# Moving P chunks, a GpSimd copy, two adds and the tail's units in a fused attention and GELU kernel on one core

## Chip, cores and metric

One core of one Trainium2 chip runs the whole kernel. The metric is the device time of an execution in microseconds (us); the kernel before has a median of 205.42 us over three runs. The engines are TensorE (PE, matrix multiply), VectorE (DVE), ScalarE (ACT), GpSimd (POOL) and SyncE (SP, which here only issues DMAs). Each engine works through its own instructions in the order in which the program issues them; semaphores order the engines against each other.

## The reference

Eight batches, eight heads of width 64, 512 tokens `x` and 32 state rows per head. The tokens read from the state and the state reads from the tokens, each through a softmax; the rows of both reads go through a two-layer network with an exact GELU.

```python
scores = x @ state.T / sqrt(D);  a  = softmax(scores);  xread = a  @ state
scores2 = state @ x.T / sqrt(D); a2 = softmax(scores2); sread = a2 @ x
y = concat([xread, sread], axis=2)          # heads side by side: (B*544, 512)
out = gelu(y @ w_in) @ w_out                # w_in 512x2048, w_out 2048x512
```

The inputs and the output (4352 x 512) are float32; matmul operands are cast to bfloat16.

## The kernel before

**The first layer.** `state @ w_in` is computed once for each batch: that is P, 256 rows (head and state row, as two halves `t` of 128) by 2048 columns. `p_mm(b, f)` makes one chunk `f` of 512 columns with eight small matmuls into two PSUM banks (L441); casts move the two halves into `Ps[b]`: `p_copy` puts one on ACT and one on DVE, `p_copy_s` both on ACT, `p_all` splits four chunks between them. The hidden layer of a batch's tokens is then `a @ P`, in 16 units M of 128 hidden columns: `mm1` (two matmuls into a bank `hp`, L506; GELU on ACT, L513, into `gs[b]`). Units 0 to 3 need chunk 0, 4 to 7 chunk 1, 8 to 11 chunk 2, 12 to 15 chunk 3.

**The second layer.** `g @ w_out` is split into 2 x 2 blocks and done with seven products in place of eight, named "1" to "7". Products 5, 6, 7 and 3 need sums of blocks of g, which `g_sum` makes on DVE (L613, tile `gsum`, from the pool `apool` of three buffers); the differences of `w_out` (`w_diff`) are made once. `X(b, name)` does one product: 16 matmuls into a PSUM bank `xp` (L623). `BANK` says which: 1, 6 and 7 accumulate in bank 1, 5 and 3 in bank 2, 2 in bank 0, 4 in bank 3. Since products share a bank, its contents are taken out in between: ACT snapshots (`snap`: c2 after 2, u after 6, s5 after 5, c4 after 4) and DVE adds (`add`, L642), which write the output tile `oh` of the upper or lower half of the tokens. After product 1 the upper half's left columns are done, after 7 both column halves of the lower one, after 3 the upper half's right columns; `x_out` sends them from SP.

**The order.** For batches 2 to 7 a loop of eight slots `p` writes the order out by hand. Each slot does two M units of batch b. Slots 0 to 3 also do products 1, 6, 5 and 7 of batch b-1. Slot 5 does product 3 of b-1, the sread matmuls of batch b (tile `sr`, L877), all four P chunks of batch b+1 (`p_all`) and product 2 of b; slot 7 does product 4 of b. Batch 2's own P is made piecemeal: chunks 0 and 1 ahead of the loop, chunk 2 in slot 0 and chunk 3 in slot 3. Slot 1 holds the scores of batch b+1, slots 2 and 3 the two halves of its softmax division (`norm`, DVE), slot 5 its transpose by DMA (`atr_dma`, SP).

**x.** `load_x` casts and loads x of a batch by a DMA issued from POOL; `hold_for` is a tiny POOL copy that waits for a GELU and so delays what follows it on POOL. From the loaded tile POOL makes two arrangements: `rearr` (L225, for the transposed x, which `xtr_dma` makes from SP) and `rearr_ones` (L235, tile `xo`, the right side of the sread matmuls). There are two `xo` buffers, for even and odd batches, and two buffers `xb`. In batch 2 `rearr_ones(3)` stands in slot 5, `load_x(5)` with its hold in slot 6, `rearr_ones(4)` in slot 7.

**The last batch.** The 256 sread rows of all batches go through both layers together, within slots of batch 7. `read_out_slot` (slots 0 to 4) does their first layer in seven products `SR` for each of two halves `g`, beside the products of batch 6; product SR("7") accumulates in the bank of SR("1") after a DVE add has read it. `R` does their second layer (L847), in slots 5 to 7 and the tail: R's 1, 6 and 7 share one bank, which before is `o1`, the home of `xp`'s bank 1. After the loop the tail does batch 7's products 1, 5 (`L5`), 6, R's 3, then 7 and 3 (`L3`). `l_mm` does 5 and 3 in three pieces in banks 2, 0 and 3, so that the last adds and output pieces can start early.

Of the kernel before, what the change touches and what calls it, by code (L numbers as in the profile page):

```python
# [17 lines left out]
def kernel(  # L18
# [8 lines left out]
    nc = tc.nc  # L27
# [202 lines left out]
    def rearr_ones(b):  # L230
        A = atts[b]
        eng = nc.vector if b < 2 else nc.gpsimd
        src = xbs[b].rearrange("p (t c) (j d) -> p t c j d", t=2, d=D)
        for t in range(2):
            eng.tensor_copy(  # L235
                out=A.xo[:, :, :, 2 + 64 * t:66 + 64 * t].rearrange("p j c d -> p c j d"),
                in_=src[:, t],
            )
# [216 lines left out]
    def pmat(b, f):  # L455
        p_copy(b, f, p_mm(b, f, ftile))
# [124 lines left out]
    xs = {}  # L581
# [53 lines left out]
    def x_out(b, h, ns=slice(None)):  # L635
        rows = out[b * SB:b * SB + S, :].rearrange("(p j) n -> p j n", j=SJ)
        nc.sync.dma_start(out=rows[:, 2 * h:2 * h + 2, ns], in_=xs[b, "o", h][:, :, ns])
# [3 lines left out]
    def add(out, x, y):  # L641
        nc.vector.tensor_tensor(out=out, in0=x, in1=y, op=ALU.add)  # L642
# [5 lines left out]
    def X(b, name):  # L648
        bank = BANK[name]
        first = name in "2154"  # L650
        if first:
            xs[b, bank] = otile([128, 2, NH], "xp", bank)
        ps = xs[b, bank]
        x_mm(ps, x_lhs(b, name), w_rhs(name), first)
        if name == "2":
            if b > 1:
                snap(b, "c2", "c2", ps)
        elif name == "4":
            snap(b, "c4", "c4", ps)
        elif name == "1":  # L660
            for h in range(2):
                xs[b, "o", h] = hpool.tile([128, 2, d_model], FP32, name="oh", tag=f"oh{h}")
            add(xs[b, "o", 0][:, :, left], ps, xs[b, "c2"])
            x_out(b, 0, left)
        elif name == "6":
            snap(b, "u", "u", ps)
        elif name == "5":
            snap(b, "s5", "s5", ps)
        elif name == "7":
            add(xs[b, "o", 1][:, :, right], ps, xs[b, "s5"])  # L670
            add(xs[b, "o", 1][:, :, left], ps, xs[b, "c4"])
            x_out(b, 1)
        elif name == "3":
            add(xs[b, "o", 0][:, :, right], ps, xs[b, "u"])
            x_out(b, 0, right)

    def rows_out(h, js, ns, eng):
        b = B - 1
# [25 lines left out]
    def L5():  # L704
        b = B - 1
        xs[b, "s5"] = c_tile("s5")
        for ps, j, n0, n1 in l_mm("5", True):
            nc.scalar.copy(out=xs[b, "s5"][:, j, n0:n1], in_=ps)

    def L3():  # L710
        b = B - 1
# [121 lines left out]
    def R(name):  # L833
        def c_new(n):
            rs[n] = cpool.tile([128, NH], FP32, name="r_" + n, tag="r_" + n)
            return rs[n]

        bank = BANK[name]
        first = name in "2154"
        if first:  # L840
            home = {"2": 1, "4": 2, "1": 1}
            rs[bank] = otile([128, NH], "rp", home[name]) if name in home else ftile([128, NH], "rp")
        ps = rs[bank]
        lhs = chain(name, r_q, {})[0] if name in "124" else rs["lhs"][name]
        rhs = w_rhs(name)
        for m in range(MH):
            nc.tensor.matmul(  # L847
                ps,
                lhsT=lhs[:, m, :],
                rhs=rhs[:, m, :],  # L850
                start=(first and m == 0),
                stop=(m == MH - 1),
                skip_group_check=True,
            )
        snaps = {"2": "c2", "4": "c4", "6": "u", "5": "s5"}
        if name in snaps:
            nc.scalar.copy(out=c_new(snaps[name]), in_=ps)
        elif name == "1":
            for h in range(2):
                rs["o", h] = opool.tile([128, d_model], FP32, name="osb", tag="osb")  # L860
            add(rs["o", 0][:, left], ps, rs["c2"])
        elif name == "7":
            add(rs["o", 1][:, right], ps, rs["s5"])
            add(rs["o", 1][:, left], ps, rs["c4"])
            r_out(1)
        elif name == "3":
            add(rs["o", 0][:, right], ps, rs["u"])
            r_out(0)
# [49 lines left out]
    def p_copy_s(b, f, ps):  # L918
        for t in range(2):
            nc.scalar.copy(out=Ps[b][:, t, f * 512:(f + 1) * 512], in_=ps[t])  # L920
# [9 lines left out]
    def M(*ms):  # L930
        for m in ms:
            mm1(m // MC, m % MC)
# [5 lines left out]
    def read_out_slot(p):  # L938
        c, b, k = B - 2, B - 1, 16 * (B - 1) + 2 * p
        if p == 0:  # L940
            sr_x("34")
            M(k, k + 1)
            g_sum(c, "56")
            SR("3", 0)
            SR("4", 0)
            X(c, "1")
            sr_x("167")
            SR("5", 0)
            SR("2", 0)
            sr_w("7")  # L950
        if p == 1:
            M(k, k + 1)
            SR_gelu("52", 0)
            X(c, "6")
            SR("1", 0)
            SR("6", 0)
        if p == 2:
            M(k, k + 1)
            SR_gelu("6", 0)
            SR("7", 0)  # L960
            SR_gelu("7", 0)
            g_sum(c, "7")
            X(c, "5")
            SR("3", 1)
            SR("4", 1)
            g_sum(c, "3")
        if p == 3:
            M(k, k + 1)
            SR("5", 1)
            SR("2", 1)  # L970
            SR_gelu("52", 1)
            X(c, "7")
            SR("1", 1)
            SR("6", 1)
        if p == 4:
            M(k, k + 1)
            SR_gelu("6", 1)
            SR("7", 1)
            SR_gelu("7", 1)
            X(c, "3")  # L980
# [146 lines left out]
    for b in range(2, B):  # L1127
        nb = b + 1
        for p in range(8):
            k = 16 * b + 2 * p  # L1130
            if p == 1 and nb < B:
                scores(nb, 0)
                scores(nb, 1)
            if p in (2, 3) and nb < B:
                norm(nb, p - 2)
            if p == 3 and nb + 1 < B:
                xtr_dma(nb + 1)
            if p == 5 and nb < B:
                atr_dma(nb)
            if nb == B and p < 5:  # L1140
                read_out_slot(p)
                if p == 4:
                    r_homes()
                    r_sum("56")
                continue
            M(k, k + 1)
            if b == 2 and p == 0:
                pmat(2, 2)
            if b == 2 and p == 3:
                p_copy_s(2, 3, p_mm(2, 3, ftile))  # L1150
            if b == 2 and p == 1:
                w_diff("7")
            if p < 5 and nb < B:
                if p == 0:
                    g_sum(b - 1, "56")
                if p == 2:
                    g_sum(b - 1, "7")
                if p == 3:
                    g_sum(b - 1, "3")
                if p < 4:  # L1160
                    X(b - 1, "1657"[p])
                if p == 1 and b > 2:
                    sr_w("5216"[b - 3])
            if p == 0 and b + 3 < B:
                hold_for(b, 0)
                load_x(4 if b == 2 else b + 3)
            if p == 6 and b == 2:
                hold_for(b, 12)
                load_x(5)
            if p == 0 and nb + 1 < B:  # L1170
                begin(nb + 1)
                rearr(nb + 1)
            if nb == B:
                if p == 5:
                    R("2")
                    r_sum("73")
                    R("4")
                if p == 6:
                    R("1")
                    X(b, "2")  # L1180
                    R("6")
                    R("5")
                if p == 7:
                    R("7")
                    X(b, "4")
                continue
            if p == 5:
                X(b - 1, "3")
                reads = (b, nb) if nb == B - 1 else (b,)
                p_all(nb, reads)  # L1190
                if b == 2:
                    rearr_ones(3)
                elif nb + 1 < B:
                    rearr_ones(nb + 1)
                X(b, "2")
            if p == 7:
                if b == 2:
                    rearr_ones(4)
                srts(reads)
                X(b, "4")  # L1200
    b = B - 1
    g_sum(b, "56")
    X(b, "1")
    g_sum(b, "73")
    L5()
    X(b, "6")
    R("3")
    X(b, "7")
    L3()


# [28 lines left out]
```

## Time and profile before

| what | value |
| --- | --- |
| time, median of three runs | 205.42 us (205.41 to 206.08) |
| the profiled execution: its time and its span | 205.37 us, 203.6 us |
| granted TensorE clock in it | 0.999 |
| busy share of DVE and ACT | 70%, 70% |
| PE on lines 623 (products) and 506 (M) in the chain that ended last | 38%, 24% |
| last matmul group, L3: start | 197.45 us |
| last output DMA issued | 199.95 us |

The span runs from the first to the last instruction in the profile; the time of the execution is 1.77 us longer. All times in the text are us from the start of the span. A timeline line gives start, duration, engine, line, operation, output<-inputs by their names, shapes and count, and in brackets the idle time of the engine before it with what ended that. Consecutive instructions of one kind are merged, and the ends of matmuls are modelled, so a group can seem to overlap the next one: the distance from start to start says more. A line of waits gives who waited for whom: total us, times, longest. The slices of time list busy time and count of PE, PE's weight loads, DVE, ACT and POOL, then PE's clock, the share of the DMA engines, and GB/s.

### The profile page before, as it was taken

The page shows a single profiled execution, that of the slowest core. Times are in us where ns is not written, and L with a number is a line of the kernel's source. Part 1 is how long each engine was busy: PE and PEld are TensorE (multiplying, and loading weights), DVE is VectorE, ACT ScalarE, POOL GpSimd, SP SyncE. Part 2 cuts the span into 40 slices and gives each one's busy share as a digit, 9 for nine tenths or more (in the row PEclk, how much of TensorE's full clock was granted, in tenths as well). Part 3 has the DMA queues.
Part 4 walks back from the last instruction along what each step waited for, and adds up shares of the span by engine and source line. Part 5 has one row for each costly group of instructions (what it writes and reads, how often), then busy time and mean ns, then how long its engine had stood idle before and what let it go on. Part 6 is the DMA issues. An engine that isn't in the chain of part 4 may idle for free.

```text
span 203.6 us, 4865 instructions
## 1 busy us (share of the span) xinstructions
PE 195.5 (96%) x2035; PEld 133.9 (66%) x2035; DVE 142.7 (70%) x233; ACT 143.3 (70%) x261; POOL 51.5 (25%) x63
## 2 busy tenths in 40 slices
PE   7899999999899999999999999999999999999991
PEld 2434544465667686677777677677766878778991
DVE  2954866788896599856895677567936787860942
ACT  3785677798976889668967796679849488654210
POOL 8963503324266095031504300300000000000000
PEclk9999999999999999999999999999999999999999
DMA  6999999978747979970797033611073010210224
GB/s 197 195 168 203 208 196 202 199 130 152 87 93 159 154 95 152 118 208 1 83 177 209 0 95 65 173 37 53 0 130 82 0 52 3 103 55 0 70 80 163
DMA packets 40166, 23.16 MB, mean 114 GB/s; under 512 B 21840, under 2 KB 38608, under 8 KB 40144
## 3 DMA queue, kind: packets, MB, share of 16 engines
q1 hardware_dynamic: 25472, 14.36, 30.5%
q0 software_dynamic: 13984, 8.10, 29.6%
q10 hardware_dynamic: 688, 0.39, 0.6%
q8 instruction: 16, 0.26, 0.5%
q14 instruction: 6, 0.05, 0.1%
HBM read 17.30 MB, written 8.91 MB: 129 GB/s over the span
## 4 chain that ended last, share of the span: by engine, by line
PE 84%; DVE 4%; DMA 4%; ACT 3%; issue 2%; DVEq 0%; POOL 0%; ACTq 0%; POOLq 0%
PE xp L623 38%; PE hp L506 24%; PE op L548 5%; PE rp L847 3%; PE sp L781 3%; DMA xb<-in_x_dram 3%; DVE oh L642 2%; PE p_ps L441 2%; PE op L532 2%; DMA st_f<-in_state_dram 2%; ACT P L915 1%; PE pt L333 1%; PE sr L877 1%; PE xp L694 1%; PE hp L1022 1%
## 5 line engine op out<-in xcount | busy, mean ns | idle before, releaser
L513 ACT ACTIVATE g<-hp 128x512 bf16<-128x512 f32 x124 | 66.0, 608 | 13.4 <-PE hp L506 13.2
L506 PE MATMUL hp<-AT,P 128*128 128x512 bf16 x248 | 61.2, 379 | 0.0
L623 PEld LDWEIGHTS <-gsum 128*128 128x128 bf16 x416 | 40.4, 98 | 10.3 <-issue 1.2
L623 PE MATMUL xp<-ws,gsum 128*128 128x256 bf16 x320 | 38.2, 273 | 0.9 <-DVE oh L642 0.9
L506 PEld LDWEIGHTS <-P 128*128 128x128 bf16 x248 | 23.4, 98 | 20.9 <-ACT P L452 0.7
L623 PEld LDWEIGHTS <-g 128*128 128x128 bf16 x336 | 32.4, 98 | 6.9 <-issue 1.9
L623 PE MATMUL xp<-w_out_bf,g 128*128 128x256 bf16 x224 | 26.7, 273 | 0.3
L235 POOL COPY xo<-xb 128x1024 bf16<-128x1024 bf16 x12 | 13.6, 1168 | 35.2 <-PE sr L877 35.2
L613 DVE TENSOR_TENSOR gsum<-g 128x2048 bf16<-128x2048 bf16 x14 | 19.0, 1355 | 0.5
L225 POOL COPY x<-xb 128x1024 bf16<-128x1024 bf16 x12 | 14.1, 1211 | 17.3 <-DMA xb<-in_x_dram 17.3
L646 ACT COPY c<-xp 128x512 f32<-128x512 f32 x14 | 8.3, 593 | 9.8 <-PE xp L623 4.5
L623 PE MATMUL xp<-ws,g 128*128 128x256 bf16 x112 | 13.4, 273 | 0.0
L915 ACT CAST P<-p_ps 128x512 bf16<-128x512 f32 x25 | 12.7, 608 | 0.1
L642 DVE TENSOR_TENSOR oh<-xp,u 128x512 f32<-128x512 f32 (+2 forms) x9 | 5.0, 569 | 10.8 <-PE xp L623 10.8
L642 DVE TENSOR_TENSOR oh<-xp,c 128x512 f32<-128x512 f32 x14 | 9.6, 685 | 4.0 <-PE xp L623 4.0
L548 PE MATMUL op<-w_out_bf,g 128*128 128x512 bf16 x48 | 11.8, 380 | 0.0
L623 PE MATMUL xp<-w_out_bf,gsum 128*128 128x256 bf16 x96 | 11.5, 273 | 0.0
L356 DVE TENSOR_TENSOR a<-e,ics 128x512 bf16<-128x512 bf16 x14 | 10.5, 750 | 0.5
L915 DVE CAST P<-p_ps 128x512 bf16<-128x512 f32 x15 | 9.4, 684 | 1.7 <-PE p_ps L441 1.7
L353 DVE TENSOR_REDUCE cs<-e 128x16 f32<-128x512 bf16 x14 | 9.5, 678 | 0.7 <-ACT e L340 0.7
L429 DVE COPY XSR<-srT 128x128 bf16<-128x128 bf16 (+1 forms) x5 | 3.4, 673 | 8.7 <-PE srT L424 8.7
L613 DVE TENSOR_TENSOR gsum<-g,gsum 128x2048 bf16<-128x2048 bf16 x7 | 9.4, 1339 | 0.0
(137 smaller groups left out, 255.4 us busy)
## 6 DMA issues: line engine op xcount, KB each, us to landing
xb<-in_x_dram POOLq DMA_DIRECT2D x7, 512.0 KB, 7.9
out_dram<-oh SPq DMA_DIRECT2D x7, 512.0 KB, 2.8
out_dram<-oh SPq DMA_DIRECT2D x13, 256.0 KB, 2.4
w_in_bf<-in_moe_w_in_dram POOLq DMA_DIRECT2D x6, 256.0 KB, 11.4
out_dram<-osb SPq DMA_DIRECT2D x5, 256.0 KB, 2.9
w_out_bf<-in_moe_w_out_dram POOLq DMA_DIRECT2D x4, 256.0 KB, 8.0
w_out_bf<-in_moe_w_out_dram POOLq DMA_DIRECT2D x2, 512.0 KB, 12.7
x0f<-in_x_dram SPq DMA_DIRECT2D x3, 256.0 KB, 4.0
```

The lines of the kernel that those rows point to most:

```text
L225: nc.gpsimd.tensor_copy(out=A.x4[:, :, :, 64 * t:64 * t + 64].rearrange("p j c d -> p c j d"), in_=src[:, t],)
L235: eng.tensor_copy(out=A.xo[:, :, :, 2 + 64 * t:66 + 64 * t].rearrange("p j c d -> p c j d"), in_=src[:, t],)
L353: nc.vector.reduce_sum(out=cs, in_=e4, axis=AX.X)
L356: nc.vector.tensor_tensor(out=A.a[:, :, hs].rearrange("p g (c n) -> p g c n", n=NS), in0=e4, in1=ics[:, :, :].to_broadcast((128, G, 2, NS) ...
L506: nc.tensor.matmul(hp, lhsT=Ps[b][:, t, m * 128:(m + 1) * 128], rhs=atts[b].AT[:, :, t, :], start=(t == 0), stop=(t == 1),)
L513: nc.scalar.activation(out=gs[b][:, m, :], in_=hp, func=AF.Gelu)
L548: nc.tensor.matmul(ops[b, j], lhsT=gs[b][:, m, j * 128:(j + 1) * 128], rhs=w_out_bf[:, m, :], start=(m == 0), stop=(m == MC - 1),)
L613: nc.vector.tensor_tensor(out=got[name], in0=x, in1=y, op=op)
L623: nc.tensor.matmul(ps[:, j - js[0], :], lhsT=lhs[:, m, 128 * j:128 * j + 128], rhs=rhs[:, m, :], start=(first and j == js[0] and m == 0), ...
L642: nc.vector.tensor_tensor(out=out, in0=x, in1=y, op=ALU.add)
L646: nc.scalar.copy(out=xs[b, name], in_=ps)
L915: copy(out=Ps[b][:, t, f * 512:(f + 1) * 512], in_=ps[t])
```

## The change

- In batch 2's loop, chunk 2 of P leaves slot 0 and chunk 3 leaves slot 3. Slot 2 now does four M units (its own and slot 3's), product 5, the second half of batch 3's `norm` (from slot 3), and then both chunks' matmuls in one run, into the four banks of the pool `f`; ACT casts the first half of each, DVE the second.
- `rearr_ones(4)` goes from slot 7 of batch 2 to slot 5, straight after `rearr_ones(3)`, ahead of `hold_for` and `load_x(5)`.
- Product 7's two adds become `c22` (right columns) and `c21` (left columns). For batches up to 5 they stand where they were. For batch 6, `c21` and the output go behind SR("1") and its add.
- The tail's order becomes 1, R's 7, 6, R's 3, 7, 5, 3. R's 7 comes from slot 7 and R's shared bank moves from `o1` to a bank of `f`. `g_sum` of 7 and 3 are issued apart. The lower half's left columns are added and sent after product 7; its right columns after each half of product 5's pieces, as two DMAs.

```diff
@@ def X
         elif name == "7":
-            add(xs[b, "o", 1][:, :, right], ps, xs[b, "s5"])
-            add(xs[b, "o", 1][:, :, left], ps, xs[b, "c4"])
-            x_out(b, 1)
+            if b < B - 2:
+                c22(b)
+                c21(b)
+                x_out(b, 1)
...
+    def c22(b, js=slice(0, 2)):
+        add(xs[b, "o", 1][:, js, right], xs[b, 1][:, js, :], xs[b, "s5"][:, js, :])
+
+    def c21(b):
+        add(xs[b, "o", 1][:, :, left], xs[b, 1], xs[b, "c4"])
@@ def L5
             nc.scalar.copy(out=xs[b, "s5"][:, j, n0:n1], in_=ps)
+            if n1 == NH:
+                c22(b, slice(j, j + 1))
+                rows_out(1, slice(j, j + 1), right, nc.sync)
@@ def R
-            home = {"2": 1, "4": 2, "1": 1}
+            home = {"2": 1, "4": 2}
@@ def read_out_slot, p == 3
             X(c, "7")
+            c22(c)
             SR("1", 1)
+            c21(c)
+            x_out(c, 1)
             SR("6", 1)
@@ the loop over slots
-            if p in (2, 3) and nb < B:
+            if p in (2, 3) and nb < B and (b > 2 or p == 2):
                 norm(nb, p - 2)
...
-            M(k, k + 1)
-            if b == 2 and p == 0:
-                pmat(2, 2)
-            if b == 2 and p == 3:
-                p_copy_s(2, 3, p_mm(2, 3, ftile))
+            if b != 2 or p != 3:
+                M(k, k + 1)
+            if b == 2 and p == 2:
+                M(k + 2, k + 3)
...
                     X(b - 1, "1657"[p])
+                if b == 2 and p == 2:
+                    norm(3, 1)
+                    for x in [(2, f, p_mm(2, f, ftile)) for f in (2, 3)]:
+                        p_copy(*x)
...
                 if p == 7:
-                    R("7")
                     X(b, "4")
                 continue
             if p == 5:
...
                 if b == 2:
                     rearr_ones(3)
+                    rearr_ones(4)
...
             if p == 7:
-                if b == 2:
-                    rearr_ones(4)
                 srts(reads)
@@ the tail
     g_sum(b, "56")
     X(b, "1")
-    g_sum(b, "73")
-    L5()
+    g_sum(b, "7")
+    R("7")
     X(b, "6")
+    g_sum(b, "3")
     R("3")
     X(b, "7")
+    c21(b)
+    x_out(b, 1, left)
+    L5()
     L3()
```

## The prediction

> **What bounds the kernel now.** I read the page's busy times first, then its chain of work, then who TensorE (PE) waited for, then the timelines of the places where it waited, and last the end.
>
> ```profile
> PE 195.5 (96%) x2035; PEld 133.9 (66%) x2035; DVE 142.7 (70%) x233; ACT 143.3 (70%) x261; POOL 51.5 (25%) x63
> ...
> PE 84%; DVE 4%; DMA 4%; ACT 3%; issue 2%; DVEq 0%; POOL 0%; ACTq 0%; POOLq 0%
> ...
> PE xp L623 <- DVE oh L642: 0.9, 2, 0.7
> PE sp L781 <- DVE srt L802: 0.2, 1, 0.2
> ```
>
> PE is busy 96% of the span and carries 84% of the chain: an edit pays only if it removes PE work, removes one of the few PE waits, or shortens what comes after PE's last matmul. Three waits stand in the loop. Each is read best from start to start, since a matmul group's end is modelled and overlaps the next group: four hp matmuls normally step 0.87 us (56.94 to 57.81).
>
> ```profile
> 53.52 1.03 PE L506 MATMUL hp<-AT,P 128*128 128x512 bf16 x4
> 55.20 1.91 PE L623 MATMUL xp<-ws,gsum 128*128 128x256 bf16 x16 [0.65 <-DVE oh L642]
> ...
> 76.05 1.03 PE L506 MATMUL hp<-AT,P 128*128 128x512 bf16 x4
> 77.33 1.91 PE L623 MATMUL xp<-ws,gsum 128*128 128x256 bf16 x16 [0.25 <-DVE oh L642]
> ...
> 174.81 1.03 PE L506 MATMUL hp<-AT,P 128*128 128x512 bf16 x4
> 176.05 0.61 PE L781 MATMUL sp<-srx,srw 128*128 128x128 bf16 x8 [0.22 <-DVE srt L802]
> ```
>
> The steps are 1.68, 1.28 and 1.24, so the losses are 0.81, 0.41 and 0.37 us: 1.59 in all. What made DVE late:
>
> ```profile
> 51.46 0.69 DVE L453 CAST P<-p_ps 128x512 bf16<-128x512 f32 x1 [1.41 <-PE p_ps L441]
> 52.07 1.21 DVE L613 TENSOR_TENSOR gsum<-g 128x2048 bf16<-128x2048 bf16 x1
> 53.32 1.23 DVE L613 TENSOR_TENSOR gsum<-gsum,g 128x2048 bf16<-128x2048 bf16 x1
> 54.46 0.68 DVE L642 TENSOR_TENSOR oh<-xp,c 128x512 f32<-128x512 f32 x1
> ...
> 72.28 3.13 DVE L613 TENSOR_TENSOR gsum<-g 128x2048 bf16<-128x2048 bf16 x1
> 72.30 2.03 POOL L235 COPY xo<-xb 128x1024 bf16<-128x1024 bf16 x2
> ```
>
> First wait: a P cast sits on DVE with 1.41 idle before it, and the two gsums and unit 1's add queue behind it. Second: gsum takes 3.13 instead of 1.22 while GpSimd (POOL) makes batch 4's xo copies, and unit 1's add is late again. Third: both adds of slot 7 (174.11 and 174.72) stand ahead of the add that frees PE's sp bank.
>
> **The change, part by part**, against the profiled execution: 205.37 us, span 203.6 and 1.77 around it (the median is 205.42, so the two are interchangeable here).
>
> *P chunk 2 leaves slot 0 of batch 2.* DVE can start gsum once the copies of L166 end (50.06): 50.06 to 52.5 for both. PE goes M 50.00, X1 50.87, scores 52.62, M 53.09, X6 at 53.96. X1 ends at 52.78, its add runs to 53.5, before 53.96. Scores need xT of batch 3, which landed 4.3 us after its issue at 47.72, at 52.0: 0.6 to spare. The wait goes: **-0.81**.
>
> *The P matmuls in one run.*
>
> ```profile
> 45.68 0.63 PE L441 MATMUL p_ps<-w_in_bf,sbd 64*32 64x512 bf16 x16
> 50.96 0.41 PE L441 MATMUL p_ps<-w_in_bf,sbd 64*32 64x512 bf16 x8
> 51.30 1.92 PE L623 MATMUL xp<-w_out_bf,g 128*128 128x256 bf16 x16
> ```
>
> A run of 8 costs 0.34 (50.96 to 51.30) and 0.09 at its entry (M steps 0.96 instead of 0.87): 0.43, twice. A run of 16 costs 0.56 (45.68 to 46.24) and 0.09: 0.65. **-0.21**.
>
> *What the crowded slot 2 must carry.* Two M steps, X5, the P run and X7 follow each other on PE at 55.71, 57.45, 59.20 and 59.85. All four f banks go to hp, then to P. ACT, from its rows: exps end 54.2, table load 1.28, GELUs 34 and 35 end 56.6, unit 6's snap 57.1, four GELUs 59.2, unit 5's snap 60.0, P casts 61.0. The run's second half wants its banks at 59.57, 0.4 after the last GELU. DVE: w_diff to 54.6, norm 1.65, gsum7 to 57.4, moved norm to 59.0 (59.8 if its multiply takes 1.51 as at 59.94), two P casts of 0.65 to 61.1 (one was ACT's), gsum3 to 62.3, or 63.1 at the 2.06 it took beside POOL at 61.37. X3 comes at 63.33 and needs it: 0.2 of cover in the worse reading. I take 0. If gsum3 takes the 3.13 of the row at 72.28 it ends at 64.1 and X3 waits 0.85; bounds 0 and +0.85. Behind gsum3 on DVE stand X7's adds, and behind these, on SP's queue, the transpose of batch 3's a: at 64.7 instead of 65.08; its 5.3 us end at 70.0, and M wants it at 71.95.
>
> *Batch 4's xo copies sooner.* Two POOL copies move past POOL's hold and its DMA issue of batch 5's x. They must wait for the sr matmuls, so run at about 65.5 to 67.5 on the new clock, beside P casts; the hold comes at about 69.9, so that DMA is not late. Even late it would have cover: the xT transpose made from it ended at 86.0, its scores ran at 97.21. What stands beside P casts is shown one batch on:
>
> ```profile
> 88.25 2.04 POOL L235 COPY xo<-xb 128x1024 bf16<-128x1024 bf16 x2 [8.04 <-PE sr L877]
> ...
> 88.94 1.29 DVE L915 CAST P<-p_ps 128x512 bf16<-128x512 f32 x2 [0.28 <-PE p_ps L441]
> ```
>
> Neither is stretched (2.04; 0.65 each), so the new place costs 0, and gsum falls from 3.13 to 1.22. Add of unit 1 then follows X1 directly, 0.5 before X6 wants it: **-0.41**.
>
> The Trainium skill (SBUF — State Buffer, "SBUF: two separate sides") says that a GpSimd instruction and a DVE one with two SBUF inputs lock each other out for one whole instruction. By that, one copy (1.0) would be the most that gsum3 could lose, it would end by 63.3, and X3 would not wait. The row at 72.28 differs: it lost 1.91, two copies, and the row decides.
>
> *Slot 7's adds parted.* Order becomes right add, SR1's add, left add, SR6's add: SR1's ends at 175.40 (174.72 + 0.68), before 175.68. **-0.37**. The left add and its 512 KB output go 0.6 later; its bank is next used at 179.11. SR6 and SR7 then add by 177.2, GELU 7 is done at 177.9, R2 wants it at 178.74.
>
> *The tail* (old clock, without what was saved). R7's eight matmuls leave 186.95 for behind X1; R1 takes an f bank, two of which are idle then. X4 186.95, X1 188.70 ends 190.61, its add 190.65 to 191.34, R7 to 191.31: X6 waits **+0.09**, starts 191.40. R3 193.15, X7 194.02 to 195.93, L5 195.77, L3 197.54.
>
> gsum3 is the fourth sum of the batch in a pool of three buffers (L45). Sum 6 is read by sum 3 itself. Before, the first to come free was sum 5's, after L5; the row agrees, since L5 ends at 193.24:
>
> ```profile
> 193.28 1.23 DVE L613 TENSOR_TENSOR gsum<-g,gsum 128x2048 bf16<-128x2048 bf16 x1
> ```
>
> Now the first to come free is sum 7's, when X7 ends. So gsum3 waits on DVE to 195.98 and ends 197.2 (L3 wants it at 197.54), and R3's add, c21 and both c22 queue behind it, until 198.86. L3's last add ends at 199.81, as PE allows. On SP: the osb output at 197.6, left half 198.3, two right rows 198.75 and 199.2, L3's rows 199.67 and 200.14.
>
> ```profile
> 199.02 0.35 SPq L637 DMA_DIRECT2D out_dram<-oh  x1
> 199.95 0.67 SPq L680 DMA_DIRECT2D out_dram<-oh  x1
> ...
> 201.80:202.00 0.20, 0.00 (x0) 0.00 (x0) 0.00 (x0) 0.00 (x0) 0.00 (x0) 1.00 0.75 213
> ```
>
> Before, 768 KB issued from 199.02 moved at some 390 GB/s with the engines full, until 202.0; the last piece landed 2.7 after its issue at 199.95, at 202.65. Now data start at about 198.85, and 1024 KB at 390 GB/s take 2.7: until 201.55, hence about 0.4 sooner; I take **-0.35**. Bounds: -0.85 if gsum3 does not wait at all (last issue 199.7, landing 2.1 as the piece issued at 192.23), +0.2 if the last piece still takes 2.7 from 200.14.
>
> The Trainium skill (DMA: Bandwidth & Descriptors, "Anatomy of one DMA") charges about 2.0 us fixed per DMA plus bytes, which speaks against cutting one output into three: by it, the last 64 KB land 2.15 after 200.14, at 202.3, still 0.35 sooner. The 64 KB row here took 2.7.
>
> Sum: -0.81 - 0.21 - 0.41 - 0.37 + 0.09 - 0.35 = -2.06; 205.37 - 2.06 = **203.3**.
>
> **Rivals.**
> *The end gains nothing*: SP issues six outputs in a row and the last goes out later than before. For it: 200.14 against 199.95. Against: the engines are no longer full then. The term is +0.1 instead of -0.35: 203.75.
> *Sum 3 takes sum 5's buffer*, as before. Then gsum3 waits for L5 (197.7), ends 198.9, L3 starts 1.4 late, and the outputs pile up: 1024 KB from 200.6 end at 203.2, landing 203.9, 1.25 later than before. -1.80 + 0.09 + 1.25: 204.9. Against: X7 ends 1.75 sooner and frees a buffer.
> *Slot 2 chokes (the other side).* POOL's four copies (57.93 to 64.33 before) hold both the moved norm's multiply and gsum3; gsum3 then starts at 64.3 and ends at 65.5, so X3 waits 2.2: 205.5, a little slower than before; it is slower from a wait of 2.1 on, and by over 0.5% from 3.1, if the copies stretch as well, as they did to 3.48. For it: DVE has about 13 us of work in the 14 between 50 and 64. Against: casts run free beside POOL.
> *It does not do what it says*: another wait stands right behind each one removed: 205.4. Against: each successor above was shown with cover.
>
> **How the numbers follow.** A measurement of this kernel tells about 0.5% (1.03 us) from no change. Forecast 0.64 (its own range 202.7 to 204.2: -0.85 in place of -0.35 and no wait of X6, or +0.85 at X3), idle end 0.14, sum 5's buffer 0.07, choke 0.09 (0.03 of it within 0.5%, 0.06 beyond), nothing 0.06. Faster 0.64 + 0.14 = 0.78; same 0.07 + 0.03 + 0.06 = 0.16; slower 0.06. The range reaches to the third case, 204.9, and leaves out 0.15.
>
> **What would show it.** X6 of batch 1 steps 0.87 behind its M; likewise X6 of batch 2 and SR7. gsum after the move is 1.22. The P run of 16 takes 0.56 and X7 follows it without a wait. X3 follows M without one. gsum3 in the tail starts as X7 ends. DMA data end under 1.9 us after the last add. The prediction is wrong if PE waits in slots 2 to 5 of batch 2 for a P cast or gsum3, or if L3 waits for gsum3.

## The result, and the profile after

The changed kernel takes 204.63 us (median of five runs, 204.41 to 204.74); the kernel before, run beside it, 206.02 (205.41 to 206.08). The ratio is 0.9947, with a 95% interval of 0.9930 to 0.9964: about 1.1 us faster, where 2.06 were forecast. (The medians lie 1.4 us apart, but the five runs of the kernel before fall near 205.4 and near 206.05, and this text goes by the ratio.) The time lies in the range given, above the likeliest case's own range. Three executions in this study ran longer than the others of their kernel (707 us for the kernel before, 208 and 406 us in two experiments); ratios and medians leave them out.

The profiled execution took 204.74 us with a span of 202.84; the kernel before has 205.37 and 203.59. First its busy times and the chain of work, from the page:

```profile
PE 194.0 (96%) x2030; PEld 134.0 (66%) x2035; DVE 140.4 (69%) x235; ACT 142.8 (70%) x260; POOL 49.9 (25%) x63
...
PE 87%; DMA 4%; POOL 4%; ACT 2%; issue 1%; DVE 0%; ACTq 0%; POOLq 0%
```

DVE's share of the chain fell from 4% to 0: the waits of PE for an add have gone. (POOL's 4% stands at the start, where the chain now passes through the issues of the first loads, 1.3 to 8.3 us.) The timeline of PE shows it at the places of the prediction (start and duration in us):

```profile
53.44 1.03 PE L506 MATMUL hp<-AT,P 128*128 128x512 bf16 x4
54.30 1.91 PE L623 MATMUL xp<-ws,gsum 128*128 128x256 bf16 x16
...
59.62 0.62 PE L441 MATMUL p_ps<-w_in_bf,sbd 64*32 64x512 bf16 x16
60.17 1.92 PE L623 MATMUL xp<-ws,gsum 128*128 128x256 bf16 x16
61.93 1.89 PE L506 MATMUL hp<-AT,P 128*128 128x512 bf16 x8
63.66 1.91 PE L623 MATMUL xp<-w_out_bf,gsum 128*128 128x256 bf16 x16
...
75.37 1.03 PE L506 MATMUL hp<-AT,P 128*128 128x512 bf16 x4
76.23 1.91 PE L623 MATMUL xp<-ws,gsum 128*128 128x256 bf16 x16
...
173.72 1.03 PE L506 MATMUL hp<-AT,P 128*128 128x512 bf16 x4
174.58 0.61 PE L791 MATMUL sp<-srx,srw 128*128 128x128 bf16 x8
...
188.97 1.04 PE L857 MATMUL rp<-ws,rs 128*128 128x256 bf16 x8
189.92 1.91 PE L623 MATMUL xp<-ws,gsum 128*128 128x256 bf16 x16
...
196.05 1.93 PE L701 MATMUL xp<-w_out_bf,gsum 128*128 128x256 bf16 x24
```

Start to start, the three steps that were 1.68, 1.28 and 1.24 us are now 0.86 each, the run of 16 takes 0.55, and in the tail product 6 follows R's 7 after 0.95.

The time is read in three stretches. Up to batch 2's first M unit (50.00 before, 50.36 after) the code is the same; over the profiles of this study that unit starts between 49.9 and 51.4, with the first loads, so this offset says nothing of the change. From there to L3's start it was 147.45 us and is 145.69: **-1.76**. From L3's start to the end of the span it was 6.14 and is 6.79: **+0.65**. The profiled executions bear this out: -1.76 + 0.65 + 0.36 at the start + 0.12 around the span is their difference of -0.63 us. (The expectations below give such lengths within 0.05 us of these, 6.75 for 6.79 for example.)

### The profile page after: what moved, and what is told of

It is laid out like the page before. It is cut to its first block, busy times and chain, and to the rows that moved or that the text cites. A ratio compares the mean times of both kernels' runs of the same rounds, so it can differ in the third digit from the quotient of the medians.

```text
span 202.8 us, 4863 instructions
## 1 busy us (share of the span) xinstructions
PE 194.0 (96%) x2030; PEld 134.0 (66%) x2035; DVE 140.4 (69%) x235; ACT 142.8 (70%) x260; POOL 49.9 (25%) x63
## 4 chain that ended last, share of the span: by engine, by line
PE 87%; DMA 4%; POOL 4%; ACT 2%; issue 1%; DVE 0%; ACTq 0%; POOLq 0%
PE xp L623 41%; PE hp L506 27%; DMA w_in_bf<-in_moe_w_in_dram 4%; PE op L548 4%; PE sp L791 3%; PE rp L857 3%; PE op L532 2%; PE xp L701 2%; PE p_ps L441 2%; PE pt L333 2%; POOL w_in_bf L105 2%; ACT P L925 1%; PE sr L887 1%; POOL sbd L95 1%; POOL w_out_bf L113 1%
## 5 line engine op out<-in xcount | busy, mean ns | idle before, releaser
L613 DVE TENSOR_TENSOR gsum<-g 128x2048 bf16<-128x2048 bf16 x14 | 17.1, 1220 | 5.1 <-ACT g L513 4.5
L225 POOL COPY x<-xb 128x1024 bf16<-128x1024 bf16 x12 | 12.4, 1066 | 18.5 <-DMA xb<-in_x_dram 18.5
L548 PE MATMUL op<-w_out_bf,g 128*128 128x512 bf16 x44 | 11.1, 380 | 0.5 <-issue 0.3
L441 PE MATMUL p_ps<-w_in_bf,sbd 64*32 64x512 bf16 x248 | 9.2, 380 | 0.2 <-DMA w_in_bf<-in_moe_w_in_dram 0.2
```

The source lines that it names most:

```text
L225: nc.gpsimd.tensor_copy(out=A.x4[:, :, :, 64 * t:64 * t + 64].rearrange("p j c d -> p c j d"), in_=src[:, t],)
L441: nc.tensor.matmul(ps[t][32 * c:32 * c + 32, :], lhsT=sbd[64 * t:64 * t + 64, b, c, 32 * t:32 * t + 32], rhs=w_in_bf[64 * t:64 * t + 64, c ...
L548: nc.tensor.matmul(ops[b, j], lhsT=gs[b][:, m, j * 128:(j + 1) * 128], rhs=w_out_bf[:, m, :], start=(m == 0), stop=(m == MC - 1),)
L613: nc.vector.tensor_tensor(out=got[name], in0=x, in1=y, op=op)
```

## The end, before and after

Before the change the 256 KB of the sread rows (`osb`) left more than a microsecond ahead of L3, as SP's timeline of the kernel before has it:

```profile
196.35 0.56 SPq L828 DMA_DIRECT2D out_dram<-osb  x1
```

In the changed kernel DVE and SP show what took its place:

```profile
194.48 1.23 DVE L613 TENSOR_TENSOR gsum<-g,gsum 128x2048 bf16<-128x2048 bf16 x1 [2.82 <-PE xp L623]
195.62 0.42 DVE L642 TENSOR_TENSOR osb<-rp,r_u 128x256 f32<-128x256 f32 x1
195.96 0.68 DVE L642 TENSOR_TENSOR oh<-xp,c 128x512 f32<-128x512 f32 x1
```

```profile
196.07 0.55 SPq L838 DMA_DIRECT2D out_dram<-osb  x1
197.12 0.39 SPq L637 DMA_DIRECT2D out_dram<-oh  x1
...
199.13 0.41 SPq L687 DMA_DIRECT2D out_dram<-oh  x1
```

DVE stands idle for 2.82 us ahead of sum 3, until product 7 has ended (194.44) and frees a buffer of `apool`; R's last add waits behind it on DVE, and so `osb` leaves at L3's start. SP then issues six outputs. The slices of time show the engines (the last two columns are the share of the 16 DMA engines and GB/s):

```profile
197.20:197.60 0.40, 0.40 (x11) 0.40 (x9) 0.40 (x3) 0.00 (x0) 0.00 (x0) 1.00 0.66 154
197.60:198.00 0.40, 0.38 (x7) 0.20 (x4) 0.26 (x2) 0.00 (x0) 0.00 (x0) 1.00 0.99 195
198.00:198.40 0.40, 0.00 (x0) 0.00 (x0) 0.29 (x1) 0.00 (x0) 0.00 (x0) 1.00 0.96 351
198.40:198.80 0.40, 0.00 (x0) 0.00 (x0) 0.00 (x0) 0.00 (x0) 0.00 (x0) 1.00 1.07 382
```

With the DMA engines full, the first part of `osb` moves at 195 GB/s or less, what follows from 198.0 on mostly at 350 to 380; the last of `osb` is among that, since the packets of 198.05 to 198.20 are still its own, of 2 KB each, and go at 314 GB/s. In all its 256 KB take about 1.1 us. It is the same where it moves alone: the 256 KB issued at 188.87 in the kernel before went at 215, 195, 174, 317 and 307 GB/s in the five slices of 0.2 us from 190.2. What makes its first part slow is not shown. The 1024 KB take from 197.2 to about 200.7, 3.5 us. Last come SP's closing row, first of the kernel after, then of the kernel before (shortest, median and longest duration in ns, first and last start in us):

```profile
L1253 SPq DRAIN  x3: 7/7/13, 202.0 to 202.3; - x3
```

```profile
L1235 SPq DRAIN  x3: 7/7/7, 202.8 to 203.1; - x3
```

Ahead of the first of these drains SP waits for each of eight DMA semaphores, in a fixed order. In the trace of the changed kernel the wait for the last piece ends at 201.50, as the first of the eight, and the seven others follow at 0.06 us each, to that drain at 201.99. In the kernel before the last piece's wait came near the end of the row: 202.63, drain at 202.76. The ledger from L3's start on, in us, with a landing read where SP's wait for it ends:

| | before | after | difference |
| --- | --- | --- | --- |
| last output issued | 2.50 | 3.08 | +0.58 |
| its landing, after that | 2.68 | 2.37 | -0.31 |
| landing to SP's drain | 0.13 | 0.49 | +0.36 |
| drain to end of span | 0.83 | 0.85 | +0.02 |
| sum | 6.14 | 6.79 | +0.65 |

## The experiments

Each ratio is to the kernel before on the same chip, with its 95% interval. Where it is said, a kernel starts from the kernel before; the others start from the changed one. Three dots in an edit stand for lines that are left out.

### The parts by themselves

**The old tail.** The changed kernel with the whole tail of before.

```diff
...
     g_sum(b, "56")
     X(b, "1")
-    g_sum(b, "7")
-    R("7")
+    g_sum(b, "73")
+    L5()
     X(b, "6")
-    g_sum(b, "3")
     R("3")
     X(b, "7")
-    c21(b)
-    x_out(b, 1, left)
-    L5()
     L3()
```

> The changed kernel with the tail as it was before the change (order, R's 7 in slot 7, adds and outputs of product 7), and the three other parts kept. Theory A/C (the loop gained all of the 1.8 us forecast and the new tail gave 0.6 back): L3's start to the end 6.15 as in the kernel before, total 0.6 to 0.7 us below the changed kernel, ratio 0.991 to 0.992. Rival E (the loop did not gain what was forecast, and the 0.36 us by which the changed kernel's profile is late at 50 us is real): ratio 0.994 to 0.996.

Measured: 203.81 us, ratio 0.9906 (0.9887 to 0.9924). L3 starts at 196.05, as in the changed kernel, and the span ends 6.10 after it, as in the kernel before (6.14). `osb` left at 194.96. Without the new tail the change is worth 1.9 us.

**The new tail alone**, from the kernel before.

```diff
...
-    g_sum(b, "73")
-    L5()
+    g_sum(b, "7")
+    R("7")
     X(b, "6")
+    g_sum(b, "3")
     R("3")
     X(b, "7")
+    c21(b)
+    x_out(b, 1, left)
+    L5()
     L3()
```

> The kernel before with the new tail alone (order, R's 7, R's bank, adds and outputs of products 7 and 5). Theory A (the new tail loses: unit 6 waits 0.08, and the end takes 0.6 longer because the osb output of 256 KB and the left and right pieces now leave in one burst behind sum 3): from L3's start to the end of the span 6.7 to 6.9 us instead of 6.1, no PE wait gone elsewhere, ratio to the kernel before 1.003 to 1.004. Rival F (the tail pays, as forecast by -0.26, and the loss lies in how it meets the new loop): 0.9985 to 0.999.

Measured: 206.63 us, ratio 1.004 (1.002 to 1.006): the tail's order costs time. Its PE timeline:

```profile
190.45 1.04 PE L857 MATMUL rp<-ws,rs 128*128 128x256 bf16 x8
191.40 1.91 PE L623 MATMUL xp<-ws,gsum 128*128 128x256 bf16 x16
```

Product 6 starts at 191.40, the prediction's very figure, and L3 at 197.53 (197.54 forecast). The rest, 6.78 us, is that of the changed kernel. So the matmuls of the tail were right and what lies behind them was not.

**The P run alone**, from the kernel before.

```diff
...
+                if b == 2 and p == 2:
+                    norm(3, 1)
+                    for x in [(2, f, p_mm(2, f, ftile)) for f in (2, 3)]:
+                        p_copy(*x)
```

> The kernel before with batch 2's third and fourth P chunk in one run in slot 2, alone. Forecast step by step: the wait of product 6 for unit 1's add goes (-0.81), one run of 16 instead of two of 8 (-0.21): -1.02 us, ratio 0.995; in the trace product 6 starts 0.87 behind its M, the run takes 0.56, product 3 follows its M without a wait. Rival G (ACT or DVE late in slots 2 to 4): PE waits 0.2 to 0.9 at the run's second half, at M of slot 4 or at product 3, ratio 0.996 to 0.9995.

Measured: 204.74 us, ratio 0.9943 (0.9921 to 0.9966).

```profile
53.26 1.03 PE L506 MATMUL hp<-AT,P 128*128 128x512 bf16 x4
54.12 1.91 PE L623 MATMUL xp<-ws,gsum 128*128 128x256 bf16 x16
...
59.44 0.62 PE L441 MATMUL p_ps<-w_in_bf,sbd 64*32 64x512 bf16 x16
59.99 1.92 PE L623 MATMUL xp<-ws,gsum 128*128 128x256 bf16 x16
```

The wait of X6 is gone, no new one stands in slots 2 to 5, and product 3 follows M at 63.48 (1.73 after its start, two M units). Slot 2 does not choke.

**GpSimd's copies alone**, from the kernel before.

```diff
                     rearr_ones(3)
+                    rearr_ones(4)
...
-                if b == 2:
-                    rearr_ones(4)
```

> The kernel before with batch 4's xo copies in slot 5 instead of 7, alone. Forecast: gsum of batch 2 takes 1.22 instead of 3.13, product 6 starts 0.87 behind its M instead of 1.28: -0.41 us, ratio 0.998. Rival H (the copies collide with the P casts or the sread norm in slot 5, or the wait is for something else): gsum is short but product 2 or 6 waits, ratio 1.0 or above.

Measured: 205.15 us, ratio 0.9966 (0.9947 to 0.9985). The timelines of DVE and PE:

```profile
72.50 1.23 DVE L613 TENSOR_TENSOR gsum<-g 128x2048 bf16<-128x2048 bf16 x1
```

```profile
76.26 1.03 PE L506 MATMUL hp<-AT,P 128*128 128x512 bf16 x4
77.12 1.91 PE L623 MATMUL xp<-ws,gsum 128*128 128x256 bf16 x16
```

The sum takes 1.23 instead of 3.13, and X6 steps 0.86.

**Slot 7's adds alone**, from the kernel before.

```diff
...
             X(c, "7")
+            c22(c)
             SR("1", 1)
+            c21(c)
+            x_out(c, 1)
             SR("6", 1)
```

> The kernel before with slot 7's two adds of batch 6 parted by SR 1's add, alone. Forecast: SR 7 starts 0.87 behind M instead of 1.24: -0.37 us, ratio 0.998. Rival I (the left add, now later, delays SR 6's and SR 7's adds, GELU 7 and with them R's 2): PE waits at R's 2 instead, ratio 1.0.

Measured: 205.16 us, ratio 0.9976 (0.9956 to 0.9995).

```profile
174.72 1.03 PE L506 MATMUL hp<-AT,P 128*128 128x512 bf16 x4
175.59 0.61 PE L788 MATMUL sp<-srx,srw 128*128 128x128 bf16 x8
```

The step is 0.87 instead of 1.24. The gains of the three parts by their ratios, 0.57, 0.34 and 0.24%, add up to 1.15% where the three together (the old tail) gave 0.94%: the same within the intervals of some 0.2% that each has. In us they are 1.2, 0.7 and 0.5, each above its steps in the timeline (1.04, 0.42 and 0.37); the intervals of some 0.4 us cover that too, and the steps are the sharper measure.

### What makes the end longer

**A fourth buffer for the sums.**

```diff
-    apool = ctx.enter_context(tc.tile_pool(name="apool", bufs=3))
+    apool = ctx.enter_context(tc.tile_pool(name="apool", bufs=4))
```

> The changed kernel with four buffers for gsum in place of three, nothing else. Theory A (the end is set by the chain of output issues on SP, which is late because sum 3 waits on DVE for product 7 and R's 3 add, the left adds and the right adds queue behind it): sum 3 starts right behind R's 7 adds, near 2.9 us sooner; the osb output leaves near 193, the last SP issue comes about 2.0 us after L3's start instead of 3.1, and from L3's start to the end of the span it takes 5.6 to 5.9 us instead of 6.75. Against the kernel before 0.989 to 0.991, where the changed kernel had 0.9947. Rival B (the end is set by the bytes still to be moved, or by a fixed time of landing and the closing barrier): sum 3 goes sooner but L3's start to the end stays within 0.2 of 6.75, and the ratio stays at 0.994 to 0.996.

Measured: 203.3 us, ratio 0.9886 (0.9864 to 0.9907). L3 starts at 196.07, as in the changed kernel, sum 3 already at 191.60, `osb` leaves at 193.21 and the span ends 5.51 after L3's start instead of 6.79. This is the case of the prediction's bound of -0.85, a sum 3 that doesn't wait: against the kernel before it gives -0.63.

**The fourth buffer in the kernel before.**

> The kernel before with four buffers for gsum, nothing else. Theory: there sum 3's wait for L5 is hidden (it starts as sum 7 ends anyway), so nothing is gained: L3's start to the end 6.1 us as before, ratio 0.999 to 1.001; the four buffers pay only with the new tail. Rival J (the fourth buffer frees gsum elsewhere too, in every batch, and that is what the changed kernel with four buffers gained): ratio 0.994 to 0.997.

Measured: 205.56 us, ratio 1.0005 (0.9989 to 1.0022). The buffer is worth nothing where the old order does not wait for it.

**R's third add ahead of sum 3**, still with three buffers.

```diff
     X(b, "6")
-    g_sum(b, "3")
     R("3")
+    g_sum(b, "3")
     X(b, "7")
```

> The changed kernel, only with sum 3 issued behind R's 3 in the tail, so that on DVE R's 3 add no longer queues behind sum 3; three buffers as before, sum 3 still waits for product 7. Theory B (the landing of the last piece is set by the bytes that must leave in one burst, and the osb output of 256 KB moves in it at only 200 GB/s with the DMA engines full): the osb output leaves near 193, the burst shrinks from 1024 to 768 KB, and the last landing comes 0.7 to 1.0 us sooner after L3's start (4.5 to 4.8 instead of 5.45); also the closing walk of waits shrinks, since the last piece on SP now has the last lane; L3's start to the end 5.5 to 5.9 instead of 6.75, ratio 0.989 to 0.991. Theory A alone (the chain of SP issues behind sum 3 and c21 sets the end): the last issue goes only 0.4 to 0.5 sooner (one step less) and so does the landing: 6.2 to 6.3, ratio 0.992.

Measured: 203.1 us, ratio 0.988 (0.9867 to 0.9893), by its ratio the lowest of the study, though the two kernels with four buffers lie within its interval. Sum 3 starts as early against L3 as in the changed kernel (1.57 ahead of it), but the add no longer queues behind it. DVE, SP and the closing row:

```profile
192.46 0.42 DVE L642 TENSOR_TENSOR osb<-rp,r_u 128x256 f32<-128x256 f32 x1 [1.07 <-PE rp L857]
...
194.20 1.23 DVE L613 TENSOR_TENSOR gsum<-g,gsum 128x2048 bf16<-128x2048 bf16 x1 [1.32 <-PE xp L623]
```

```profile
192.91 0.55 SPq L838 DMA_DIRECT2D out_dram<-osb  x1
196.06 0.39 SPq L637 DMA_DIRECT2D out_dram<-oh  x1
...
198.06 0.40 SPq L687 DMA_DIRECT2D out_dram<-oh  x1
```

```profile
L1253 SPq DRAIN  x3: 7/7/13, 200.3 to 200.6; - x3
```

From the first M unit of batch 2 to L3's start it takes 145.69 us, just as in the changed kernel. After L3's start SP's last issue comes at 2.29 instead of 3.08, it lands 1.96 after that instead of 2.35 (by the semaphore's last update), and the span ends at 5.39 instead of 6.79. The closing row is as long as it was (0.50), but it now begins with ACT's last piece, which landed at 199.80; SP's own, landed at 200.02, is waited for near its end, so that 0.29 us pass from there to the drain. So the queue on SP, the bytes in flight and the place in the row were all paid for, and each costs less with `osb` sent early. This run doesn't part them, but the share of the DMA engines points to the one that bound: in the changed kernel it is 0.86 to 1.11 in each 0.4 us from 197.6 to 200.4, so there the bytes set the landing, more than the issues; here it falls to 0.77 and 0.74 between 198.4 and 199.2, where pieces issued 0.5 us apart no longer fill the engines.

**The same output from ACT's queue**, behind L5, which takes one issue from SP and leaves the bytes.

```diff
...
-            r_out(0)
...
     L5()
+    r_out(0, nc.scalar)
     L3()
```

> The changed kernel, but the osb output behind R's 3 (256 KB) is issued from ACT, behind L5's three snapshots, instead of SP. Theory A (issues on SP follow each other at 0.5 us and the one behind an osb output at 1.05): the left half's output leaves as its add ends, 0.45 us sooner, all SP issues after it as well, and L3's start to the end is 6.3 to 6.4 instead of 6.75; ratio 0.992 to 0.993. Rival B (bytes in flight set the end): the same bytes, no gain, 6.7 or more, ratio 0.9947.

Measured: 205.15 us, ratio 0.9982 (0.9965 to 0.9998): worse than the changed kernel, a miss for both expectations. L3 starts at 196.32 in its profile. Two queues' timelines, and SP's closing row:

```profile
196.58 0.72 ACTq L838 DMA_DIRECT2D out_dram<-osb  x1
```

```profile
196.94 0.38 SPq L637 DMA_DIRECT2D out_dram<-oh  x1
...
199.43 0.41 SPq L687 DMA_DIRECT2D out_dram<-oh  x1
```

```profile
L1253 SPq DRAIN  x3: 7/7/7, 202.8 to 203.1; - x3
```

SP's last issue is no sooner (3.11 after L3's start against 3.08), though it has one less: a hole takes its place. `osb` itself, issued 0.24 later against L3 and in 0.72 instead of 0.55, is later: its bytes begin 1.64 after L3's start instead of 1.23, and the last piece lands 0.5 later (5.94 against 5.45). With the same last issue the landing follows the bytes ahead of it.

**Batch 4's upper half in one output**, so that SP has one DMA fewer and the eight semaphores fall otherwise.

```diff
-            x_out(b, 0, left)
+            if b != 4:
+                x_out(b, 0, left)
...
-            x_out(b, 0, right)
+            x_out(b, 0, right if b != 4 else slice(None))
```

> The changed kernel, but batch 4's upper half is sent in one output DMA behind product 3 instead of two, so that every later DMA of the hardware queues takes the semaphore one place earlier, and the last piece on SP has the last of the eight in SP's closing row of waits instead of the first. Theory C (behind the last landing SP still has to walk the other waits, 0.06 us each): from the last landing to SP's drain 0.1 instead of 0.5, L3's start to the end of the span about 6.35 instead of 6.75, ratio about 0.993. Rival D (the walk costs nothing, something else holds the end): 6.75 and 0.9947 unchanged.

Measured: 204.53 us, ratio 0.9942 (0.9923 to 0.9961), no gain. The last issue and the closing row:

```profile
198.78 0.96 SPq L688 DMA_DIRECT2D out_dram<-oh  x1
```

```profile
L1254 SPq DRAIN  x3: 7/7/13, 201.7 to 202.0; - x3
```

The walk did shrink from 0.49 to 0.06 us, but the last issue took 0.96 instead of 0.41 and the landing came at 6.01 after L3's start instead of 5.45, so what was won was lost again.

**Both: R's third add first, and one output fewer.**

> The changed kernel with sum 3 issued behind R's 3, and batch 4's upper half sent in one output DMA, so that the last piece on SP and the last on ACT hold the last two of the eight semaphores in SP's closing row of waits. Theory C (after the last landing SP still walks the waits that stand behind it, 0.06 us each): from the last landing to SP's drain 0.1 to 0.15 us instead of 0.5, L3's start to the end 4.9 to 5.0 instead of 5.35, ratio 0.986. Rival D (as the first lane experiment could be read: what the walk gives, a later landing takes back): the walk is short, but the last landing comes 0.3 or more later after L3's start than 4.04, and the ratio stays at 0.988.

Measured: 203.70 us, ratio 0.9903 (0.9871 to 0.9935), not better than the third add alone. The walk is 0.12, but on SP a hole and an issue of 0.78 us put the last issue at 2.98 after L3's start instead of 2.29.

**Four buffers, and one of the two right rows issued from ACT.**

```diff
-                rows_out(1, slice(j, j + 1), right, nc.sync)
+                rows_out(1, slice(j, j + 1), right, nc.scalar if j else nc.sync)
```

> Four buffers for gsum, and in addition the second of the two right-column outputs is issued from ACT, which is idle between L5's snapshots and its own last issue. Theory A (with four buffers the last SP issue, 2.45 us after L3's start, sets the landing): the last SP issue goes to 2.0 us or less after L3's start, the end to 5.0 to 5.2 us after it instead of 5.47; ratio 0.986 to 0.987. Rival (the last add, 2.26 us after L3's start, and ACT's issue behind it set the end, or bytes do): 5.4 to 5.5, ratio 0.9886 as with four buffers alone.

Measured: 203.07 us, ratio 0.9884 (0.9866 to 0.9903), as with four buffers alone. SP's last issue goes out at 1.97 after L3's start, but ACT's own last one goes at 2.29 and then sets the end at 5.30.

## Why the prediction was right, and where it failed

*The loop's terms* were right to 0.05 us. The steps give 0.82, 0.22, 0.42 and 0.38 us gained where 0.81, 0.21, 0.41 and 0.37 were forecast, and the tail's 0.95 step gives +0.08 for the +0.09; the sum, -1.76 against -1.71, is what the trace has between the first M unit and L3. The covers held as well: product 3 waits for nothing (M at 61.93, product 3 at 63.66). Sum 3 of slot 3 lost 0.56 us beside POOL's copies (1.78 instead of 1.22), less than one of them. The Trainium skill (SBUF — State Buffer, "SBUF: two separate sides") says that whichever of the two instructions starts first holds the shared ports for its whole length; it doesn't say which comes next when a second copy stands ready. So "one copy would be the most" was the prediction's own step: the 0.56 here keeps to it, the 1.91 of the row at 72.28, beside copies of 2.03 in all, is what two copies in a row would cost.

*The step that failed is the term for the end*, "I take **-0.35**": it is +0.65. Its mechanism was foreseen: that sum 3 waits for product 7, that R's third add and so `osb` queue behind it, that six outputs leave one after the other and that 1024 KB move at the end. So the order of events was right and its price was not. By the sum the landing was to come 4.83 us after L3's start (5.18 before, less 0.35) and came at 5.45: 0.62 late. Closing then took another 0.36 that no term of the sum had, and from the drain on it took 0.02 more, which makes the 1.00 of the miss. The sizes that were wrong:

- The rate. 390 GB/s was read from a stretch in which only outputs of `oh` moved, and from its faster half: its 768 KB, from about 199.85 to 202.0, make some 365. `osb` took 1.1 us for its 256 KB, some 240 GB/s, and the other 768 KB about 2.35, some 335, with a dip at 198.8 to 199.2. So 1024 KB took 3.5 us, not 2.7. Whoever reads a rate has to ask which transfer it belongs to.
- SP's issues. The left half was to go 0.76 after L3's start and went at 1.07, because SP did nothing for about 0.45 us after its inputs were ready (c21 had ended at 196.64); and each further issue steps 0.50, not 0.45 to 0.47. The last one went 3.08 after L3's start, not 2.60.
- The closing row of waits: 0.49 us instead of 0.13.

The bound of +0.2 rested on SP's last issue at 200.14 and on the same 0.13; its 2.7 for the landing was enough (2.37). A smaller slip is that the times of the end stand on a clock that already has the 0.09 of product 6, which the sum adds once more.

*The rivals.* "The end gains nothing" names the right place and the right mechanism (SP issues six in a row), but its +0.1 was too small by over half a microsecond. "Sum 3 takes sum 5's buffer" did not happen: sum 3 starts 0.04 after product 7 ends. "Slot 2 chokes" is refuted by product 3, which follows its M without a wait, and "It does not do what it says" by the steps of 0.86.

*On the fixed price of a DMA.* The prediction weighed the Trainium skill (DMA: Bandwidth & Descriptors, "Anatomy of one DMA"), about 2.0 us fixed and the bytes on top, 2.15 for 64 KB, against a row of 2.7. That section treats DMAs that GpSimd issues; these outputs go from SP and ACT, so the rule was carried over. The last piece took this long:

```profile
out_dram<-oh SPq DMA_DIRECT2D x1, 64.0 KB, 2.4
```

The 64 KB outputs of the study landed 1.7 to 3.3 us after their issue, the short ones where less was in flight ahead of them, and 256 KB sent with nothing ahead of them landed after 2.1 (issued at 192.23 before the change), where the rule gives 2.6. So for these outputs the rule is no floor, and what is queued ahead of the piece comes on top.

## What to carry to other kernels

When an order is changed near the end, list every output with its bytes and the moment it leaves, before and after: an output that slips from ahead of the last matmuls into the last burst costs an issue and its bytes there, though no matmul waits. A small add that sends something off belongs ahead of an instruction that waits for a buffer, not behind it; by the ratios (0.9947 to 0.988) swapping two lines here was worth about 1.4 us, as much as another buffer (0.9886) within the intervals. And a rate read from one transfer need not hold for another.

## Of the hardware, not expected

- **A hole on SP.** In the changed kernel SP stood still for about 0.45 us, with inputs ready, before issuing `x_out`. In five of the profiles it stands ahead of the 80th of SP's instructions in the trace (0.45 or 0.46 us): that is the same output in the new tail alone, and the output behind it in the three kernels where SP has an earlier output less (batch 4's, or `osb` on ACT). In the nine others SP waits 1.46 to 2.54 us for an add at that place anyway. What it is was not shown.
- **Long issues.** In the last 15 us an issue of `oh` on SP mostly takes 0.34 to 0.53 us and one of `osb` 0.55 to 0.68. Single ones of `oh` took longer: 0.67 for the last piece in all six kernels with the old tail, 0.78 to 1.21 in four of those with the new one. The cause is open.
- **The closing row** of eight waits has a fixed order, so which semaphore the last output has is worth up to 0.43 us (0.06 or 0.49). To shift it by one output moved the hole too, and no version here won by it.
- **A hold beside a sum.** POOL's hold ahead of batch 4's load took 0.19 us before; in the changed kernel a sum on DVE runs from 51.71 to 52.94, and the hold ends with it:

```profile
51.78 1.20 POOL L937 COPY hold<-g 128x1 bf16<-128x1 bf16 x1 [1.41 <-ACT g L513]
```

  It made batch 4's load 0.6 us later against the first M unit (2.56 after it instead of 1.93), which PE did not wait for.
